# Chunk-selected attention followed by a gated FFN: a hand-merged order against one computed at build time, with VectorE 32x32 transposes in place of TensorE transposes

## The chip, the cores and the metric

The kernel runs on one core of one Trainium2 chip. Times are device microseconds (us) of one execution. "Busy", "waited for" and the chain of waits come from the hardware profile of one execution. Engines in the profile: PE is TensorE's matmuls, PEld its weight loads, DVE is VectorE, ACT is ScalarE, POOL is GpSimd, SP only issues loads and stores. Verdicts come from timed runs taken in turn with the kernel before on the same chip.

## The reference, cut to what matters

Four batches, 8 heads, 768 positions, head size 64. For every query only six of the 24 key chunks (32 keys each) are kept. They are those with the largest upper bound, which is computed from each chunk's minimum and maximum. Attention output goes into a gated FFN.

```python
k_min, k_max = k_chunks.min(3), k_chunks.max(3)          # chunks of 32 keys
ub = sum(max(q * k_min, q * k_max), axis=-1)             # upper bound per query and chunk
ub = where(causal, ub, -1e9);  top = argsort(ub)[..., -6:]
scores = where(selected & (pos_q >= pos_k), q @ k.T / 8, -1e9)
x = softmax(scores) @ v                                   # to (4*768, 512)
out = (sigmoid(x @ w_gate) * (x @ w_val)) @ w_out         # 512 -> 1536 -> 512
```

## The kernel before

The work is cut into eight units: batch 0 to 3, each with a first half "a" and a second half "b" of the queries (384 each). In this text "0b" is the second half of batch 0. Each unit needs preparation (k and q turned so that the head dimension lies on partitions, chunk extremes, bounds, selection), attention, and then the FFN. Preparation of the next unit and the FFN of the previous one are woven into a unit's attention by hand-set fractions; the first unit has a fully hand-written order.

```python
pff = tile_pool(bufs=3, space=PSUM)   # FFN
psc = tile_pool(bufs=3, space=PSUM)   # scores and values
ppr = tile_pool(bufs=2, space=PSUM)   # preparation

def keys_t(u, p, pool, tag="ps"):     # two heads: [positions, 2 x 64] turned by TensorE, fp32
    ps = pool.tile([128, T], F32, ...)
    for x in range(HB):
        nc.tensor.transpose(ps[:, x:T:HB], u.k[:, x, 2*p:2*p+2, :]..., ident32)

def extremes(u, p): ...               # two tensor_reduce per pair, straight from PSUM
def signs(u, p, eng): ...             # max(q,0) and max(-q,0), an own copy for each head
def bounds(u, j):                     # four heads: TensorE into PSUM, ScalarE copies out
def pick(u, j):                       # TensorE turns the bounds (fp32), VectorE: penalty, max8, is_lt
def pick_t(u, j, eng):                # TensorE turns the mask back (fp16), copies into headQ rows 64..95

def score(u, h, x, ...):              # keys carry 32 pattern rows, queries 32 mask rows
    nc.tensor.matmul(ps, headK[...][:, h, ...], headQ[...][:, h, ...])     # 96 rows
    nc.scalar.activation(at, ps, AF.Exp, scale=scale)
    if x == 0: nc.gpsimd.affine_select(...)                                # causal triangle

def merge(a, f):                      # FFN pieces of the previous unit go in by fractions of time
    for c, t in a:
        t(); done_a += c
        while fi < len(f) and done_f + f[fi][0] / 2 <= tf * done_a / ta: ...
# ... cut: opening(), a fixed sequence of about 100 calls for units 0a and 0b
```

The softmax here doesn't subtract the row's maximum and nothing guards it: scores larger than these inputs give would overflow.

Of the kernel before, what the change touches and what calls it, by code (L numbers as in the profile page):

```python
# [14 lines left out]
NEG = -60000.0  # L15


@with_exitstack
def kernel(
# [11 lines left out]
    ctx.enter_context(tc.manual_schedule(engines={nc.gpsimd.engine, nc.sync.engine}))  # L31
# [5 lines left out]
    T = 128 * HB  # L37
    NP = H // 2
# [4 lines left out]
    consts = ctx.enter_context(tc.tile_pool(name="consts", bufs=1))  # L43
    keep = ctx.enter_context(tc.tile_pool(name="keep", bufs=1))
    loads = ctx.enter_context(tc.tile_pool(name="loads", bufs=2))
    nat = ctx.enter_context(tc.tile_pool(name="nat", bufs=1))
    sel = ctx.enter_context(tc.tile_pool(name="sel", bufs=1))
    ubp = ctx.enter_context(tc.tile_pool(name="ubp", bufs=2))
    attp = ctx.enter_context(tc.tile_pool(name="attp", bufs=4))
    small = ctx.enter_context(tc.tile_pool(name="small", bufs=3))  # L50
    xnatp = ctx.enter_context(tc.tile_pool(name="xnatp", bufs=2))
    xtp = ctx.enter_context(tc.tile_pool(name="xtp", bufs=2))
    gatep = ctx.enter_context(tc.tile_pool(name="gatep", bufs=3))
    hglp = ctx.enter_context(tc.tile_pool(name="hglp", bufs=18))
    outp = ctx.enter_context(tc.tile_pool(name="outp", bufs=3))
    PS = bass.MemoryType.PSUM
    pff = ctx.enter_context(tc.tile_pool(name="pff", bufs=3, space=PS))
    psc = ctx.enter_context(tc.tile_pool(name="psc", bufs=3, space=PS))
    ppr = ctx.enter_context(tc.tile_pool(name="ppr", bufs=2, space=PS))

    class Unit:
        def __init__(self, b, half):
            self.b, self.half = b, half
            self.name = f"{b}{'ab'[half]}"
            self.qa, self.qb = HB * half, HB * half + HB
            self.rows = slice(T * half, T * half + T)
            self.sel0 = 1 - half
            self.m = HB - self.sel0
            self.paired = b == 0
            self.cb = T // CH * (half + 1)  # L70
            self.banks = HIGH if half else LOW
            self.where = {}
            base = 0
            for bk in self.banks:
                for (jb, i0, n) in bk:
                    for o in range(0, n, 128):
                        self.where[((i0 + o) // 128, jb)] = base + o
                    base += n
            self.width = base
            self.att, self.pv, self.kps, self.qps, self.ubT = {}, {}, {}, {}, {}  # L80
# [10 lines left out]
    ]  # L91
    units = [Unit(b, half) for b in range(B) for half in range(2)]

    def load(u):
        for n, src in (("k", k), ("q", q)):
            t = loads.tile([128, H, HB, D], F32, tag="raw" + n, name=f"raw{n}_{u.name}")
            for j in range(2):
                nc.sync.dma_start(t[:, 4 * j:4 * j + 4], src[u.b, 4 * j:4 * j + 4, u.rows].rearrange(  # L98
                    "h (p x) d -> p h x d", x=HB))
            setattr(u, "raw" + n, t)  # L100
        u.v = loads.tile([128, HB, H, D], F32, tag="v", name=f"v_{u.name}")
        for i in range(HB):
            r = T * u.half + 128 * i
            nc.sync.dma_start(u.v[:, i], v[u.b, :, r:r + 128].rearrange("h p d -> p h d"))  # L104

    def regroup(u, n, parts):
        raw = getattr(u, "raw" + n)
        if not hasattr(u, n):
            setattr(u, n, nat.tile([128, HB, H, D], F32, tag=n, name=f"{n}_{u.name}"))
        t = getattr(u, n)  # L110
        for f, h0, h1 in parts:
            f(t[:, :, h0:h1, :], raw[:, h0:h1].rearrange("p h x d -> p x h d"))  # L112

    ident32 = consts.tile([128, 128], F32, tag="id32")
    ident16 = consts.tile([128, 128], F16, tag="id16")
    epat = consts.tile([32, NC, CH], F16, tag="epat")
    NQ = 2 * HB - 1
    pen = consts.tile([128, NQ, NC], F32, tag="pen")
    kmx = keep.tile([128, NP, 2, 32], F32, tag="kmx", name="kmx")
    kcat, v16s, apt, headK, headQ = [], [], [], [], []  # L120
    for i in range(2):
        kcat.append(keep.tile([128, H, 32], F32, tag=f"kcat{i}", name=f"kcat{i}"))
        headK.append(keep.tile([96, H, S], F16, tag=f"hk{i}", name=f"hk{i}"))
        headQ.append(keep.tile([96, H, T], F16, tag=f"hq{i}", name=f"hq{i}"))
        apt.append(keep.tile([128, HB, 4, 32], F16, tag=f"ap{i}", name=f"ap{i}"))
        v16s.append(keep.tile([128, 2 * HB, H, D + 1], F16, tag=f"v16{i}", name=f"v16{i}"))

    def fill_pattern(i, eng):
        eng.dma_start(headK[i][64:96],
                      epat.rearrange("p c s -> p (c s)").unsqueeze(1).to_broadcast([32, H, S]))  # L130

    def constants():
        make_identity(nc, ident32)
        nc.vector.memset(epat, 0.0)
        nc.gpsimd.affine_select(
            out=epat, in_=epat, compare_op=ALU.not_equal, fill=NEG,
            base=0, pattern=[[-1, NC], [0, CH]], channel_multiplier=1,
        )
        fill_pattern(0, nc.sync)
        nc.vector.memset(kmx, 0.0)  # L140
        nc.vector.memset(pen, 0.0)
        nc.gpsimd.affine_select(
            out=pen, in_=pen, compare_op=ALU.is_ge, fill=-1e9,
            base=128, pattern=[[128, NQ], [-CH, NC]], channel_multiplier=1,
        )
        for i in range(2):
            nc.vector.memset(kcat[i], 0.0)
            nc.vector.memset(apt[i], 0.0)
            nc.gpsimd.memset(v16s[i][:, :, :, D:D + 1], 1.0)
        nc.vector.memset(headQ[0][64:96, :, 0:128], 0.0)  # L150
        nc.vector.tensor_copy(ident16, ident32)

    wg16 = keep.tile([128, 4, D_FF], F16, tag="wg16")
    wv16 = keep.tile([128, 4, D_FF], F16, tag="wv16")
    wo16 = keep.tile([128, NFB, 512], F16, tag="wo16")
# [4 lines left out]
    def load_w(i):  # L160
        lo, hi = 512 * i, 512 * i + 512
        nc.gpsimd.dma_start(wg16[:, :, lo:hi], wgs[:, :, lo:hi])  # L162
        nc.gpsimd.dma_start(wv16[:, :, lo:hi], wvs[:, :, lo:hi])

    def load_wo(i):
        nc.gpsimd.dma_start(wo16[:, 4 * i:4 * i + 4, :], wos[:, 4 * i:4 * i + 4, :])

    def cast_v(u):
        nc.gpsimd.tensor_copy(v16s[u.b % 2][:, u.qa:u.qb, :, 0:D], u.v)  # L169

    def keys_t(u, p, pool, tag="ps"):
        if p == 0:
            if u.paired:
                u.kmm = kmx[:, :, :, T // CH * u.half:T // CH * (u.half + 1)]
            else:
                u.kmm = sel.tile([128, NP, 2, T // CH], F32, tag="kmm", name=f"kmm_{u.name}")
        ps = pool.tile([128, T], F32, tag=tag, name=f"kT_{u.name}_{p}")
        for x in range(HB):
            nc.tensor.transpose(ps[:, x:T:HB],  # L179
                                u.k[:, x, 2 * p:2 * p + 2, :].rearrange("p h d -> p (h d)"), ident32)  # L180
        u.kps[p] = ps

    def extremes(u, p):
        pv = u.kps[p].rearrange("p (c s) -> p c s", s=CH)
        for e, op in enumerate((ALU.max, ALU.min)):
            nc.vector.tensor_reduce(out=u.kmm[:, p, e, :], in_=pv, op=op, axis=AX.X)  # L186

    def chunks_t(u, j):
        c0 = T // CH * u.half
        for e in range(2):  # L190
            for i, sign in enumerate((1.0, -1.0)):
                nc.vector.tensor_scalar_mul(kcat[u.b % 2][64 * i:64 * i + 64, 4 * j + e:4 * j + 4:2, c0:c0 + T // CH],  # L192
                                            u.kmm[64 * e:64 * e + 64, 2 * j:2 * j + 2, i, :], sign)

    def keys_f(u, p, eng):
        ps = u.kps.pop(p)
        for e in range(2):
            eng(headK[u.b % 2][0:64, 2 * p + e, u.rows], ps[64 * e:64 * e + 64])  # L198

    def queries_t(u, p, pool, tag="ps"):  # L200
        if p == 0:
            u.qs = sel.tile([128, H, T], F32, tag="qs", name=f"qs_{u.name}")
        ps = pool.tile([128, T], F32, tag=tag, name=f"qT_{u.name}_{p}")
        for x in range(HB):
            nc.tensor.transpose(ps[:, x:T:HB],
                                u.q[:, x, 2 * p:2 * p + 2, :].rearrange("p h d -> p (h d)"), ident32)
        u.qps[p] = ps
# [373 lines left out]
```

## Time and profile before

Median of the first three runs: 357.51 us (355.94 to 359.78).

| reading | value |
|---|---|
| profiled span | 353.9 us |
| PE busy | 316.5 us, 89% |
| ACT, DVE, POOL busy | 234.4, 216.4, 74.1 us |
| PE busy in the first 60 us | 41.4 us |

The page's part 1 gives busy time, share and instructions of each engine; part 2 cuts the span in 40 slices and gives the busy share in tenths; part 4 gives the chain that ended last, by engine.

```profile
span 353.9 us, 7200 instructions
PE 316.5 (89%) x2736; PEld 197.0 (56%) x2736; DVE 216.4 (61%) x642; ACT 234.4 (66%) x501; POOL 74.1 (21%) x106
...
PE   4678687999988999999987999999998999999995
...
DVE  6576548985667569864776469883585574322430
...
DMA  8999992057900066001740039001100020001002
...
PE 54%; ACT 16%; issue 10%; DVE 8%; DMA 5%; SPq 4%; POOL 2%; ACTq 0%; POOLq 0%; DVEq 0%
```

The windows view gives busy us in each stretch, with the granted TensorE clock and the DMA engines' share.

```profile
core 0: us, PE busy (x) PEld busy (x) DVE busy (x) ACT busy (x) POOL busy (x), PEclk, DMA share, GB/s
0.00:60.00 60.00, 41.38 (x332) 26.50 (x333) 37.77 (x124) 35.12 (x76) 21.74 (x35) 0.94 1.04 211
60.00:340.00 280.00, 265.11 (x2359) 165.81 (x2358) 177.20 (x516) 196.53 (x420) 52.34 (x72) 1.00 0.23 63
340.00:354.00 14.00, 10.03 (x50) 4.69 (x48) 1.43 (x3) 2.77 (x5) 0.00 (x0) 0.95 0.15 56
```

The timeline of PE, around the first FFN matmul of unit 0a and the first scores of unit 0b (start, duration, engine, line, operation):

```profile
30.40 0.33 PE L330 MATMUL g_0a_512<-xT_0a,wg_120 128*128 128x384 f16 x1
...
55.67 0.39 PE L289 MATMUL sc_0b_0_777<-hq_117,hk_111 96*128 96x128 f16 x4
```

PE is the limit, yet busy PE is not streaming PE. Matmuls overlap and wait while they count as busy: one of 128x384 counts 326 ns, but the next can start 162 ns after it. I therefore count streaming (the time that the matmuls would take one right behind the other) by the medians of start-to-start times (162 ns for a 128x384 matmul, 216 for 128x512, 29 for 128x65, 110 for an fp32 transpose). By that estimate about 286 of the 354 us are streaming. The first 60 us hold 30 us of it.

### The profile page before, as it was taken

The page shows a single profiled execution, that of the slowest core. Times are in us where ns is not written, and L with a number is a line of the kernel's source. Part 1 is how long each engine was busy: PE and PEld are TensorE (multiplying, and loading weights), DVE is VectorE, ACT ScalarE, POOL GpSimd, SP SyncE. Part 2 cuts the span into 40 slices and gives each one's busy share as a digit, 9 for nine tenths or more (in the row PEclk, how much of TensorE's full clock was granted, in tenths as well). Part 3 has the DMA queues.
Part 4 walks back from the last instruction along what each step waited for, and adds up shares of the span by engine and source line. Part 5 has one row for each costly group of instructions (what it writes and reads, how often), then busy time and mean ns, then how long its engine had stood idle before and what let it go on. Part 6 is the DMA issues. An engine that isn't in the chain of part 4 may idle for free.

```text
span 353.9 us, 7200 instructions
## 1 busy us (share of the span) xinstructions
PE 316.5 (89%) x2736; PEld 197.0 (56%) x2736; DVE 216.4 (61%) x642; ACT 234.4 (66%) x501; POOL 74.1 (21%) x106
## 2 busy tenths in 40 slices
PE   4678687999988999999987999999998999999995
PEld 3265345656554566655664466665665456665552
DVE  6576548985667569864776469883585574322430
ACT  4683467787888475876789375884789467665321
POOL 3393204211420040210421032201421011110000
PEclk9979999999999999999999999999999999999999
DMA  8999992057900066001740039001100020001002
GB/s 223 268 207 224 232 226 49 0 163 198 267 3 0 31 199 130 2 0 62 222 77 0 32 113 215 3 0 52 41 0 2 0 87 4 2 3 59 31 0 89
DMA packets 50642, 31.13 MB, mean 88 GB/s; under 512 B 26032, under 2 KB 47536, under 8 KB 50608
## 3 DMA queue, kind: packets, MB, share of 16 engines
q1 hardware_dynamic: 45856, 25.96, 28.2%
q0 software_dynamic: 4752, 4.72, 7.8%
q8 instruction: 21, 0.34, 0.4%
q14 instruction: 13, 0.11, 0.1%
HBM read 28.31 MB, written 6.29 MB: 98 GB/s over the span
## 4 chain that ended last, share of the span: by engine, by line
PE 54%; ACT 16%; issue 10%; DVE 8%; DMA 5%; SPq 4%; POOL 2%; ACTq 0%; POOLq 0%; DVEq 0%
DMA v_0b<-in_v_dram 5%; SPq L104 2%; ACT hq_117 L236 2%; SPq L98 1%; ACT hq_112 L236 1%; ACT qs_2b L227 1%; ACT qs_3b L227 1%; ACT qs_1b L227 1%; ACT hk_116 L198 1%; PE o_2b_4225 L345 1%; PE o_1b_2989 L345 1%; PE o_1a_2399 L345 1%; ACT qs_1a L227 1%; PE o_2a_3645 L345 1%; PE o_0b_1743 L345 1%
## 5 line engine op out<-in xcount | busy, mean ns | idle before, releaser
L336 PEld LDWEIGHTS <-wv_121 128*128 128x128 f16 x384 | 37.0, 97 | 38.4 <-issue 16.6
L330 PEld LDWEIGHTS <-wg_120 128*128 128x128 f16 x384 | 35.2, 98 | 16.1 <-issue 1.9
L289 PEld LDWEIGHTS <-hk_111 96*128 96x128 f16 x240 | 19.7, 101 | 13.0 <-issue 8.2
L289 PEld LDWEIGHTS <-hk_116 96*128 96x128 f16 x240 | 19.2, 97 | 9.4 <-issue 3.1
L179 PE MATMUL kT_0a_172<-ident_105,k_0a 128*128 128x128 f32 x3 | 0.9, 430 | 4.9 <-DVE k_0a L112 4.9
L295 POOL TENSOR_SCALAR_AFFINE_SELECT att_0b_776<-att_0b_776 128x384 f16<-128x384 f16 x1 | 0.5, 515 | 19.7 <-ACT att_0b_776 L292 19.7
L179 PEld LDWEIGHTS kT_0a_172<-ident_105,k_0a 128*128 128x128 f32 x3 | 0.5, 213 | 4.8 <-issue 4.8
L277 ACT COPY hq_117<-apT_0b_735 32x384 f16<-32x384 f16 x4 | 1.9, 469 | 1.8 <-PE apT_0b_735 L273 1.8
L112 ACT COPY k_0a<-rawk_0a 128x384 f32<-128x384 f32 x2 | 1.0, 512 | 2.9 <-DMA rawk_0a<-in_k_dram 2.9
L192 DVE TENSOR_SCALAR kcat_110<-kmm_2b 64x24 f32<-64x24 f32 x8 | 2.8, 350 | 0.1
L192 DVE TENSOR_SCALAR kcat_115<-kmm_3b 64x24 f32<-64x24 f32 x8 | 2.8, 350 | 0.1
L313 DVE RECIPROCAL rz_3b_4888<-pv_3b_4849 128x6 f32<-128x6 f32 x1 | 0.2, 196 | 4.3 <-PE pv_3b_4849 L309 4.3
L277 DVE COPY hq_112<-apT_3a_3801 32x256 f16<-32x256 f16 x4 | 1.2, 288 | 2.7 <-PE apT_3a_3801 L273 2.7
L277 DVE COPY hq_112<-apT_2a_2555 32x256 f16<-32x256 f16 x4 | 1.2, 288 | 2.7 <-PE apT_2a_2555 L273 2.7
L169 POOL CAST v_114<-v_0b 128x1536 f16<-128x1536 f32 x1 | 1.5, 1465 | 6.1 <-DMA v_0b<-in_v_dram 6.1
L313 DVE RECIPROCAL rz_1b_2434<-pv_1b_2339 128x6 f32<-128x6 f32 x1 | 0.2, 196 | 4.0 <-PE pv_1b_2339 L309 4.0
L313 DVE RECIPROCAL rz_2b_3680<-pv_2b_3585 128x6 f32<-128x6 f32 x1 | 0.2, 197 | 4.0 <-PE pv_2b_3585 L309 4.0
L273 PEld LDWEIGHTS <-ap_118 128*128 128x128 f16 x20 | 1.7, 98 | 1.5 <-DVE ap_118 L267 0.2
L162 POOL DMA_DIRECT2D wg_120<-in_moe_w_gate_dram x3 | 2.4, 808 | 0.0
L348 ACT ACTIVATE osb_3b_5093<-o_3b_5080 128x512 f32<-128x512 f32 x1 | 0.6, 597 | 2.8 <-PE o_3b_5080 L345 2.8
L198 ACT CAST hk_111<-kT_0b_494 64x384 f16<-64x384 f32 x2 | 0.9, 474 | 2.2 <-DVE kmx L186 2.2
L169 POOL CAST v_114<-v_0a 128x1536 f16<-128x1536 f32 x1 | 1.5, 1469 | 4.4 <-DMA v_0a<-in_v_dram 4.4
(1976 smaller groups left out, 1085.3 us busy)
## 6 DMA issues: line engine op xcount, KB each, us to landing
wg_120<-in_moe_w_gate_dram POOLq DMA_DIRECT2D x3, 512.0 KB, 8.9
wv_121<-in_moe_w_val_dram POOLq DMA_DIRECT2D x3, 512.0 KB, 12.0
wo_122<-in_moe_w_out_dram POOLq DMA_DIRECT2D x3, 512.0 KB, 13.6
rawk_0a<-in_k_dram SPq DMA_DIRECT2D x2, 384.0 KB, 3.8
rawq_0a<-in_q_dram SPq DMA_DIRECT2D x2, 384.0 KB, 5.2
v_0a<-in_v_dram SPq DMA_DIRECT2D x3, 256.0 KB, 6.3
rawk_0b<-in_k_dram SPq DMA_DIRECT2D x2, 384.0 KB, 6.3
rawq_0b<-in_q_dram SPq DMA_DIRECT2D x2, 384.0 KB, 6.5
```

The costliest lines, as they stand in the source:

```text
L98: nc.sync.dma_start(t[:, 4 * j:4 * j + 4], src[u.b, 4 * j:4 * j + 4, u.rows].rearrange("h (p x) d -> p h x d", x=HB))
L104: nc.sync.dma_start(u.v[:, i], v[u.b, :, r:r + 128].rearrange("h p d -> p h d"))
L169: nc.gpsimd.tensor_copy(v16s[u.b % 2][:, u.qa:u.qb, :, 0:D], u.v)
L192: nc.vector.tensor_scalar_mul(kcat[u.b % 2][64 * i:64 * i + 64, 4 * j + e:4 * j + 4:2, c0:c0 + T // CH], u.kmm[64 * e:64 * e + 64, 2 * j:2 ...
L198: eng(headK[u.b % 2][0:64, 2 * p + e, u.rows], ps[64 * e:64 * e + 64])
L227: nc.scalar.activation(o, src, AF.Relu, scale=sign)
L236: eng(headQ[u.half][0:64, 2 * p + e, :], ps[64 * e:64 * e + 64])
L277: eng(headQ[u.half][64:96, 4 * j + i, s0:T], ps[32 * i:32 * i + 32, s0:T])
L289: nc.tensor.matmul(ps[:, o:o + w], headK[u.b % 2][:, h, 128 * jb:128 * jb + 128], headQ[u.half][:, h, i:i + w], start=True, stop=True)
L330: nc.tensor.matmul(gp, wg16[:, c, 128 * fb:128 * fb + 128], u.xT[:, c, :], start=(c == 0), stop=(c == 3))
L336: nc.tensor.matmul(vp, wv16[:, c, 128 * fb:128 * fb + 128], u.xT[:, c, :], start=(c == 0), stop=(c == 3))
L345: nc.tensor.matmul(op, hgl[(u.name, fc)][:, 128 * tb:128 * tb + 128], wo16[:, fc, :], start=(fc == 0), stop=(fc == NFB - 1))
```

## The change

It keeps the arithmetic and replaces how the work is ordered and turned.

1. Every operation is put into a plan with its reads, writes, buffers, possible engines and a cost for each. At build time a simulation of the engines picks what is issued next, and on which engine. The eight PSUM banks are shared by need.
2. Head p is paired with head p+4. Bounds of eight heads are computed at once into two banks.
3. The selection is turned by VectorE 32x32 block transposes instead of TensorE.
4. In batches 2 and 3 k and q are loaded as 32x32 blocks in 128-byte runs and turned by VectorE. Batches 0 and 1 still use TensorE.

The core of it, cut:

```diff
-    pff = tile_pool(bufs=3)   psc = tile_pool(bufs=3)   ppr = tile_pool(bufs=2)
+    plan = Plan({"ps": 8, "big": 2, "six": 4, ...},
+                {("ps", "ff"): 4, ("ps", "sc"): 3, ("ps", "pv"): 2, ("ps", "pr"): 3})
+def act(n, psum=True, parts=128): took = (170 if psum else 195) + n / 1.2; ...
+def dve(n, rate=1, parts=128):    took = 158 + n / 0.96 / rate; ...
+def pool(n):                      took = 190 + n / 1.2; ...
+  def order(self):     # earliest possible start first, then rank
+      key = (s > free[e], s if s > free[e] else 0.0, op.prio)
+    self.wide = b <= 1                      # batches 2 and 3: blocks
-    nc.tensor.transpose(ps[:, x:T:HB], u.k[...], ident32)
+    nc.vector.transpose(at(u.qf)[:, p], at(raw)[:, p, c0:c0 + NT]...)     # 32x32 blocks
+    nc.vector.tensor_reduce(out, src, op, axis=AX.X, apply_transpose=True)
-    nc.tensor.transpose(ps[...], u.ubT[j][...], ident32)                  # selection
+    nc.vector.transpose(at(ubn)[:, e_]..., at(ub[e_]))
+    hkp{i}{e_}: {DVE: (880, 960)} if i == 0 else {POOL: (2700, 2750)}     # pattern rows into the keys
-    fill_pattern(i): eng.dma_start(headK[i][64:96], epat...)
+    hqm: {POOL: pool(u.n), DVE: dve(u.n, 4, 32), ACT: act(u.n, False, 32)}  # mask rows into the queries
+    for op in plan.order(): op.emit(op.engine)
  # ... cut: the classes, constants, loads, attention and FFN written as plan entries
```

## The prediction

> **What bounds the kernel now.** The tensor engine. The page gives PE 316.5 us busy of a 353.9 us span (89%), against ACT 234.4, DVE 216.4, POOL 74.1; the chain that ended last is 54% PE. From the medians of start-to-start times in the trace (gate and value matmuls 128x384: 162 ns; output 128x512: 216; values 128x65: 29; fp32 transposes 110; fp16 transposes 55) I count about 286 us of pure streaming for all 2736 matmuls (an estimate; FFN alone 186). So about 68 us are lost: some 29 us in the first 60 us (windows view: PE 41.4 busy, granted clock 0.94, DMA engines saturated; POOL waits 19.7 us for the first 0b scores, which start only at 55.7 us, long after 0a's FFN began), some 36 us over 60-340 us (PE 265 busy of 280, about 244 streaming), 4 us in the tail.
>
> **What leaves PE** (estimates from those pitches): k and q transposes of batches 2 and 3, 96 x 109 ns = 10.5 us; selection's transposes, 40 x 110 + 40 x 55 ns = 6.6 us; the bounds stay near 10 us. Streaming falls to about 268 us. FFN, scores and values stay.
>
> **Other engines.** DVE loses sign splits, chunk sign copies and key casts, and gets 32x32 transposes, which I cost like its other ops of one element per cycle (549 ns at 384). It ends near 170 us fixed work plus a share of copies. The Trainium skill ("VectorE: DVE Perf Modes", The three transpose paths) says that this transpose turns 32x32 blocks only and goes to SBUF; no run shows its time yet. ACT keeps about 166 us that cannot move (exp 105, tanh 47, output 14). POOL roughly doubles, to 130-170 us. None becomes the bound. A risk: "GPSIMD Engine Reference" (Key points) says that POOL shares its SBUF interfaces with VectorE in two-port modes, so POOL copies might stretch (now 1.46 us for 1536).
> DMA: batch 2-3 k and q come in 128-byte runs, 49,152 packets; from 22 ns at 256 B and 36 ns at 768 B I estimate 18 ns each, 55 us of all 16 engines, at 100-250 us where they are mostly idle.
>
> **Order.** Half or more of the gain should come from order: PSUM banks shared as needed, copies on whichever engine is free, 0b's attention beginning when its data is there. I expect the first 60 us to lose 22 instead of 29, and the steady part 22 instead of 36, since real waits differ from the model's fixed costs; tail 4. Sum: 268 + 22 + 22 + 4 = 316; 2 more for POOL and DVE collisions.
>
> **Prediction: 318 us, 302 to 338 with 8 chances in 10.** Faster by over 2%: 0.94; within 2%: 0.03; slower: 0.03.
>
> **What would show the steps.** Matmuls drop from 2736 to about 2650, fp32 transposes from 232 to 96. From 60 us on PE is busy over 95%. 0b's first scores start before 45 us. POOL over 120 us. DVE transposes near 0.5 us per 384 columns. 128-byte packets near 18 ns.
>
> **What would make it wrong.** In-order queues obey an order computed from fixed costs: where a POOL copy or a DMA is late, PE stalls behind it and the gains of order vanish (335-345). DVE could bind if transposes are slower than one element per cycle. If the order nearly fills PE from 25 us on, 300 is possible. The start could be worse, since the first selection now needs eight heads' keys and queries.

## The result, and the profile after

The changed kernel took 319.65 us (median of four; 319.46 to 320.87). The kernel before took 356.73 us beside it. The ratio is 0.8961, with a 95% interval of 0.8917 to 0.9004. A ratio here is the mean time of one kernel's fast runs over that of the other's of the same rounds, so not quite the ratio of the medians quoted.

The same lines of the page:

```profile
span 317.8 us, 7014 instructions
PE 289.7 (91%) x2656; PEld 181.5 (57%) x2656; DVE 198.9 (63%) x568; ACT 206.4 (65%) x440; POOL 104.1 (33%) x171
...
PE   3577789989999949999998999999999999999995
...
DVE  8988694498868999678999617432675213321420
...
DMA  7999999704999357998410010000200010002002
...
PE 63%; DVE 19%; ACT 11%; issue 3%; DMA 2%; POOL 1%; SPq 0%; ACTq 0%; DVEq 0%; POOLq 0%
```

The windows view, and the timeline of PE around the same two matmuls:

```profile
0.00:60.00 60.00, 44.78 (x360) 28.04 (x361) 45.47 (x137) 44.07 (x97) 32.31 (x51) 0.94 1.11 232
60.00:304.00 244.00, 234.75 (x2251) 148.73 (x2249) 151.86 (x429) 159.59 (x339) 71.81 (x120) 0.99 0.36 64
304.00:318.00 14.00, 10.18 (x51) 4.76 (x49) 1.58 (x3) 2.77 (x5) 0.00 (x0) 0.98 0.16 57
```

```profile
40.90 0.65 PE L679 MATMUL g_0a<-xT_0a,wg 128*128 128x384 f16 x3
...
47.04 0.55 PE L593 MATMUL sc_0b<-hqe,hke 96*128 96x128 f16 x5
```

Three things are to be seen. From 60 us to the tail PE is busy 234.75 of 244 us (96%, before 95%). More of it is streaming: by the same count 275 us in all, of which 33 lie in the first 60 us and 228 in the 240 us from 60 to 300. In the last ten slices but the very last PE is simply full, while VectorE is down to 0 to 5 tenths. But the start has hardly gained: 33 us of streaming in 60 us against 30. Unit 0b's scores begin 9 us earlier, and 0a's FFN begins 10 us later. VectorE now stands in the chain of waits with 19% instead of 8%.

The VectorE transposes cost what other fp32 work of that size costs on VectorE: in the same trace its reductions of 384 columns from PSUM take 547 ns in the mean (groups by form; after the first bar stand the busy us of the group and the mean ns of one):

```profile
L489 DVE STREAM_TRANSPOSE kt<-k 128x768 f16<-128x768 f16 x8 | 7.6, 944 | 0.0
...
L503 DVE STREAM_TRANSPOSE qf_2a<-q 128x384 f32<-128x384 f32 x4 | 2.1, 552 | 0.0
```

### The profile page after: what moved, and what is told of

Its sections match the earlier page's. It is cut to its first block, busy times and chain, and to the rows that moved or that the text cites. A ratio compares the mean times of both kernels' runs of the same rounds, so it can differ in the third digit from the quotient of the medians.

```text
span 317.8 us, 7014 instructions
## 1 busy us (share of the span) xinstructions
PE 289.7 (91%) x2656; PEld 181.5 (57%) x2656; DVE 198.9 (63%) x568; ACT 206.4 (65%) x440; POOL 104.1 (33%) x171
## 4 chain that ended last, share of the span: by engine, by line
PE 63%; DVE 19%; ACT 11%; issue 3%; DMA 2%; POOL 1%; SPq 0%; ACTq 0%; DVEq 0%; POOLq 0%
PE o_2a L700 2%; PE o_1b L700 2%; PE v_3a L679 2%; PE g_3a L679 2%; PE g_2a L679 2%; PE v_2a L679 2%; PE v_3b L679 2%; PE g_3b L679 2%; PE o_3b L700 2%; PE o_2b L700 2%; PE o_3a L700 2%; PE g_0a L679 2%; PE v_0a L679 2%; PE v_2b L679 2%; PE g_2b L679 2%
## 5 line engine op out<-in xcount | busy, mean ns | idle before, releaser
L679 PEld LDWEIGHTS <-wv 128*128 128x128 f16 x384 | 36.4, 98 | 21.7 <-issue 1.8
L679 PEld LDWEIGHTS <-wg 128*128 128x128 f16 x384 | 35.1, 97 | 17.9
L593 PEld LDWEIGHTS <-hke 96*128 96x128 f16 x240 | 19.3, 101 | 13.5 <-issue 7.5
L593 PEld LDWEIGHTS <-hko 128*128 128x128 f16 x240 | 18.6, 99 | 7.5 <-DVE x_0a L648 0.8
L607 ACT ACTIVATE att_1b<-sc_1b 128x512 f16<-128x512 f32 (+1 forms) x32 | 16.7, 578 | 1.7 <-PE sc_1b L593 1.6
L607 ACT ACTIVATE att_3b<-sc_3b 128x512 f16<-128x512 f32 (+1 forms) x32 | 17.0, 580 | 1.2 <-PE sc_3b L593 1.2
L607 ACT ACTIVATE att_2b<-sc_2b 128x512 f16<-128x512 f32 (+1 forms) x32 | 17.0, 580 | 0.9 <-PE sc_2b L593 0.8
L607 ACT ACTIVATE att_0b<-sc_0b 128x512 f16<-128x512 f32 (+1 forms) x32 | 16.5, 625 | 0.9 <-PE sc_0b L593 0.7
L679 PE MATMUL g_0a<-xT_0a,wg 128*128 128x384 f16 x48 | 9.9, 326 | 0.1
L700 PE MATMUL o_0b<-wo,hg_0b 128*128 128x512 f16 x36 | 9.9, 435 | 0.0
L613 POOL TENSOR_SCALAR_AFFINE_SELECT att_3a<-att_3a 128x384 f16<-128x384 f16 x8 | 4.2, 521 | 17.6 <-ACT att_3a L607 17.5
```

Source lines behind the costliest of these rows:

```text
L593: nc.tensor.matmul(at(t)[:, o:o + w], hk[u.par][e_][USED[e_], p, 128 * jb:128 * jb + 128], hq[u.half][e_][USED[e_], p, i:i + w], start=Tru ...
L607: plan.add(f"exp_{u.name}_{h}_{x}", {ACT: act(n)}, lambda e, t=t, att=att, b0=b0, n=n: nc.scalar.activation(at(att)[:, b0:b0 + n], at(t), ...
L613: nc.gpsimd.affine_select(out=dv, in_=dv, compare_op=ALU.is_ge, fill=0.0, base=0, pattern=[[0, HB], [1, 128]], channel_multiplier=-1)
L679: nc.tensor.matmul(at(t), w16[:, c, 128 * fb:128 * fb + 128], at(u.xt)[:, c, :], start=(c == 0), stop=(c == 3))
L700: nc.tensor.matmul(at(o), at(hgs[fc])[:, 128 * tb:128 * tb + 128], wo16[:, fc, :], start=(fc == 0), stop=(fc == NFB - 1))
```

## The experiments

Twelve kernels ran, all correct. They answer three questions: how the gain divides between less TensorE work and order, which part of the ordering carries it, and why the start did not gain.

### 1. Less work or better order: undo the work alone

The three edits keep the simulated order. The first puts batches 2 and 3 back on TensorE (with the four large buffers under names of their own, since sharing them left the plan no way on). The second writes the selection with TensorE transposes again. The third does both.

```diff
# x1_pe_layout
-            self.wide = b <= 1
+            self.wide = b <= 3
-  "six": 4                      + "kn": 1, "qn": 1, "qf": 1, "qm": 1
# x2_pe_select (cut; per bank of four heads, as in the kernel before)
-  nc.vector.transpose(ubn, ub)                 # from PSUM, 32x32 blocks
+  copy(ubt, ub);  for x in range(m): nc.tensor.transpose(ubp[...], ubt[...], ident32)
-  nc.vector.transpose(apt, ap)
+  for x in range(m): nc.tensor.transpose(apt[...], apq[...][:, x], ident16)
# x3_pe_both: both edits
```

> The changed kernel with one part undone: batches 2 and 3 get their k and q layout by TensorE transposes again, like batches 0 and 1; order still from the build-time simulation. Theory of the prediction (work on the tensor engine is worth its streaming time): 96 fp32 transposes x 109 ns = 10.5 us more, so about 330 us. Rival 'worth more' (the block layout mostly relieves the other engines and PSUM): 336 us or more. Rival 'order is all' (the tensor engine has slack to take it): 322 us or less.

> The changed kernel with the selection turned by TensorE again: bounds copied out of PSUM, 40 fp32 transposes, bounds and maxima as before, 40 fp16 transposes, mask rows from PSUM; order still from the simulation. Theory of the prediction: 6.6 us of streaming, so about 326 us. Rival 'worth more': 330 us or more. Rival 'order is all': 321 us or less.

> Both parts undone at once: all of the tensor engine's removed transposes are back, only the simulated order, the shared PSUM banks, the free choice of engine and the pairing of heads remain of the change. Theory of the prediction (work worth 17 us, order worth 20): about 337 us. Rival 'worth more': over 345 us, order alone brings little. Rival 'order is all': under 326 us.

| run | median us | ratio to before (95%) | what it undoes |
|---|---|---|---|
| the change | 319.65 | 0.8961 (0.8917 to 0.9004) | |
| x1_pe_layout | 325.38 | 0.9099 (0.9034 to 0.9164) | layout: 5.7 us |
| x2_pe_select | 325.56 | 0.9104 (0.9044 to 0.9165) | selection: 5.9 us |
| x3_pe_both | 335.38 | 0.9377 (0.9322 to 0.9433) | both: 15.7 us |

With all removed TensorE transposes back, 21.6 of the gain remain (356.97 less 335.38). So order and what comes with it (shared banks, free engines, pairing, finer copies) is worth about 22 us, and the removed transposes about 16. Both rivals fall: order is not all, and work is not worth far more than its streaming. The layout alone, though, cost only 5.7 us to undo where 10.5 us of streaming came back. The windows of the two traces show where the rest was; each first number is PE busy, the third DVE busy, in the same 20 us. First the change, then x1_pe_layout:

```profile
100.00:120.00 20.00, 15.82 (x138) 8.67 (x136) 19.86 (x60) 11.69 (x27) 8.59 (x14) 0.98 0.54 121
```

```profile
100.00:120.00 20.00, 19.77 (x176) 11.98 (x173) 17.95 (x62) 12.32 (x30) 8.27 (x17) 1.00 0.69 181
```

In the change VectorE is full there (19.86 of 20 us), about half of it with batch 2's keys and queries, and PE stands idle for 4 us; with TensorE doing that layout PE is full. That is a reading of two traces; experiment 4 tests it.

### 2. Which part of the ordering carries the gain

```diff
# x4_by_rank: same operations, next one by fixed rank alone; engine that would end it first
-  best = earliest possible start over all engines, then rank
+  best = lowest rank of all operations whose buffers are free
# x5_static_psum
-  {"ps": 8, ...}, caps ff 4, sc 3, pv 2, pr 3
+  {"ff": 3, "sc": 3, "pr": 2, ...}             # scores and values share the middle three
# x6_flat
+  engines = {e: (400, 500) for e in engines}    # one cost for everything but loads
# x7_fixed_engine
+  if len(engines) > 1: engines = {ACT or DVE in turn: its cost}
```

> The changed kernel, same operations, but emitted by fixed rank alone (the interleaving by fractions that feeds the simulation), without regard to simulated readiness; each operation still goes to the engine that would end it first. If the simulated readiness is what fills the tensor engine: clearly slower than the change, 345 us or more. If finer pieces, shared banks and fewer transposes suffice: about 325 us.

> The changed kernel with the eight PSUM banks split fixedly as before (3 for the FFN, 3 for scores and values, 2 for preparation), order re-simulated under that limit. If sharing banks is a large part of what order brings: 328 us or more. If the order itself carries the gain: within 3 us of the change, 319 to 323 us.

> The changed kernel ordered by the same simulation, but with every operation given the same cost (400 ns busy, 500 ns to its end) on every engine; loads keep their modelled times. If the measured costs in the model matter: 330 us or more. If knowing only what waits for what, with ranks and free engines, suffices: within 5 us of the change.

> The changed kernel with each movable copy put to a fixed engine, ScalarE and VectorE in turn (VectorE or ScalarE alone where it can't be the other), none on GpSimd where ScalarE or VectorE can do it; order simulated with that. If the free choice of engine is a large part: 330 us or more. If not: 320 to 325 us; it could even gain, since GpSimd then collides less with VectorE.

| run | median us | ratio to before (95%) |
|---|---|---|
| x4_by_rank | 363.79 | 1.0169 (1.0101 to 1.0238) |
| x5_static_psum | 326.58 | 0.9130 (0.9067 to 0.9193) |
| x6_flat | 345.09 | 0.9622 (0.9553 to 0.9691) |
| x7_fixed_engine | 321.99 | 0.8986 (0.8928 to 0.9044) |

The same operations by fixed rank are 44 us slower than the change, and 1.7% slower than the kernel before with all its extra work (interval 1.0 to 2.4%). In that trace PE waits for single late copies, up to 8.4 us for one, and what was emitted behind it waits too; in the change its longest single wait is 4.2 us (who waited for whom, total us, times, longest):

```profile
PE xps_2a L641 <- DVE x_2a L633: 10.1, 4, 8.4
PE sc_0b L578 <- DVE hqe L237: 5.5, 1, 5.5
```

So fewer transposes and finer pieces brought nothing under this order; an order that knows when inputs are ready is needed to collect them. (The rank order is not the hand-made order of before, which was tuned; the run doesn't say what that order lacked.) Knowing only what waits for what is not enough either: flat costs lose 25 us. Part of both losses may lie in the clock. Its mean in the profiled executions is 0.939 with the rank order and 0.949 with flat costs, against 0.983 in the change. The shortfall from full clock, times the span, is 22, 18 and 5 us, so by an estimate at most 17 of the 44 us and 12 of the 25 us lie there; whether the order brought the lower clock about was not tested. Sharing the banks is worth some 7 us; this lies between the two figures expected, so it is a real but not a large part. Free choice of engine is worth little: 2.3 us in the medians, and the intervals of the ratios overlap.

### 3. Why the start did not gain

In the change two long GpSimd copies run at the start. They write the chunk pattern into the keys of the odd batches, which are needed only at 80 us. VectorE's timeline of the change beside GpSimd's; the second column is the duration:

```profile
8.66 0.97 DVE L453 TENSOR_TENSOR kcr<-kx_0a,kcr 128x12 f32<-128x12 f32 x1
...
10.49 1.94 DVE L453 TENSOR_TENSOR kcr<-kx_0a,kcr 128x12 f32<-128x12 f32 x1
```

```profile
6.87 2.74 POOL L254 COPY hke<-epat 32x3072 f16<-32x3072 f16 x1
9.67 2.74 POOL L254 COPY hko<-epat 64x3072 f16<-64x3072 f16 x1
```

A subtraction of 12 elements takes 0.15 to 0.16 us with no GpSimd work beside it (x8_late_fill below, at 8.54 and 9.60). During the copies it took 0.97 and 1.94 us, and it ended at 9.63 and 12.43 us, within 0.03 us of the copies' ends (9.61 and 12.41). The Trainium skill ("SBUF — State Buffer", SBUF: two separate sides) describes this: VectorE and GpSimd share one pair of ports under an exclusive lock, held for a whole instruction, against VectorE ops with two SBUF inputs or in a two-port mode. This trace agrees. The other side can wait too: in x8_late_fill a GpSimd copy of 384 elements that began during a VectorE copy of the pattern (5.18 to 6.56 us) took 1.32 us, where others of its kind take 0.51. In the change both subtractions stand in the chain that ended last, with 2.75 us together (start, us, what):

```profile
8.75 0.89 DVE kcr L453
...
10.57 1.86 DVE kcr L453
```

```diff
# x8_late_fill
-  hkp1: two GpSimd copies of 3072 elements, as soon as GpSimd is free
+  hkp1: eight copies of 768 elements, after unit 0b's values are cast
# x10_late_noqm: x8, and
-  qm of batches 2 and 3: {DVE, ACT, POOL: pool(2 * u.n)}
+  qm of batches 2 and 3: {DVE, ACT}
# x11_recal: x10, and four VectorE costs from the trace of the change
-  hqm: dve(u.n, 4, 32)    kcr: dve(n)        hk: dve(S, 4, 64)      qm: dve(2 * u.n, 2)
+  hqm: dve(u.n, 1.55, 32) kcr: (257, 337)    hk: dve(S, 2.37, 64)   qm: dve(2 * u.n)
# x0_control: the change, unedited
```

> The changed kernel once more, unedited, as the yardstick on this chip for the three runs beside it: 319.7 us as before, within 1 us.

> The changed kernel, but the two long GpSimd copies of the chunk pattern into the keys of odd batches (2.7 us each, at 6.9 and 9.7 us) are cut in eight and wait until the values of unit 0b are cast, some 20 to 40 us later; the model's order of all else stays the same. Theory (two VectorE subtractions of 12 elements took 0.97 and 1.94 us because they waited for those copies): each ends near 0.15 us, the first selection comes 2 to 3 us earlier, and the whole is 2 to 3 us faster. Rival (the start hangs on loads or on the selection's length): no change beyond 1 us.

> As the run before, and GpSimd may not take the maxima with zero of the queries of batches 2 and 3, which took it 1.5 and 2.1 us where the model says 0.6 and 0.8. One of these stood in the chain of waits at 126.8 us. Theory: 1 to 2 us faster than the run before. Rival (slack takes it up): no change.

> As the run before, and four VectorE costs of the model set to the means measured in the trace of the change (mask rows 417 ns for 384 columns instead of 268, the 12-element subtraction 337 instead of 170, half-partition fp16 key copies 495 instead of 368, maxima of queries at one element per cycle). Theory (the model's optimism about VectorE makes it overload VectorE between 60 and 160 us): 2 to 4 us faster than the run before. Rival (the shape of the order matters, not its numbers): within 1 us.

| run | median us | ratio to before (95%) |
|---|---|---|
| x0_control | 320.99 | 0.8985 (0.8958 to 0.9012) |
| x8_late_fill | 313.22 | 0.8767 (0.8733 to 0.8801) |
| x10_late_noqm | 312.74 | 0.8767 (0.8740 to 0.8794) |
| x11_recal | 309.34 | 0.8670 (0.8645 to 0.8696) |

Moving two copies brought 7.8 us in the medians, more than the 2 to 3 us expected. The profiled spans, 317.8 and 312.7, differ by only 5.1 us, but they pair an execution of the change at a clock of 0.983 with the slowest one of x8_late_fill, at 0.978. At like clocks, 0.987 to 0.988, the control took 319.52 us and x8_late_fill 311.36 and 310.78. The control came out 1.3 us above its earlier median, a little outside what was expected of it. The four subtractions of unit 0a all took 0.15 to 0.16 us, three of them here:

```profile
8.54 0.15 DVE L454 TENSOR_TENSOR kcr<-kx_0a,kcr 128x12 f32<-128x12 f32 x1
...
9.60 0.16 DVE L454 TENSOR_TENSOR kcr<-kx_0a,kcr 128x12 f32<-128x12 f32 x1
...
11.12 0.16 DVE L454 TENSOR_TENSOR kcr<-kx_0a,kcr 128x12 f32<-128x12 f32 x1
```

The mask of unit 0a is turned at 19.0 us instead of 23.2, 0a's FFN starts at 36.3 instead of 40.9, and 0b's scores at 43.0 instead of 47.0. PE's timeline of x8_late_fill shows the last two:

```profile
36.34 0.50 PE L680 MATMUL g_0a<-xT_0a,wg 128*128 128x384 f16 x2
...
43.00 0.38 PE L594 MATMUL sc_0b<-hqe,hke 96*128 96x128 f16 x4
```

In the profiled executions that gain of 4 to 5 us is kept to the end. By the chain above about 2.4 us of it is the wait of the two subtractions (2.75 less two of 0.16; an estimate). Part of the rest is that GpSimd, now free, took five of the eight early copies of 0a's k and q, where it had taken one and ScalarE seven. So the run shows what the two copies cost, but does not split their lock from GpSimd's time.

One thing more differs at the start, and no run isolates it. The first fp32 transposes on PE start 213 ns apart, later ones 109. The slow rate ends at 7.8 us in the kernel before and near 12 us in x8_late_fill, but only at about 20 us in the change, where the bounds of 0a ran at it too (0.63 us each, against 0.38 to 0.40). The clock column does not show this. It may be a part of the start's loss, and of x8_late_fill's gain.

Keeping GpSimd from the query maxima gave nothing, so that the chain passed through one of them was not a cost. They are slow on GpSimd all the same (instructions of that source line in the change; duration in ns, min, median, max):

```profile
L477 POOL TENSOR_SCALAR qm_2a<-qf_2a x1: 1496/1496/1496, 120.0 to 120.0; 128x512 f32<-128x512 f32 x1
L477 POOL TENSOR_SCALAR qm_2b<-qf_2b x1: 2126/2126/2126, 126.8 to 126.8; 128x768 f32<-128x768 f32 x1
```

Correcting four costs in the model to what the trace of its own kernel shows brought another 3.4 us in the medians. About 1 us of that may be clock: x10_late_noqm had 0.973 to 0.978 in five of its six executions, x11_recal 0.987 to 0.994 in all, and at 0.987 they took 311.85 and 309.33 us. In the profiled executions of x8_late_fill and x10_late_noqm the clock is at half for 6.8 us from 111 us on, in x11_recal it is not; whether the better costs avoid that was not tested. The four costs were changed together; which of them counts is not known.

### 4. Was the VectorE layout held back by the order?

```diff
# x12_recal_pe_layout: x11_recal with
-            self.wide = b <= 1
+            self.wide = b <= 3
```

> The recalibrated run (309.3 us) with the layout of batches 2 and 3 back on TensorE. Undoing that part cost the unedited change only 5.7 us for 10.5 us of streaming. Theory: the VectorE layout paid for itself only in part there, because VectorE was the bound around 100 to 120 us under the optimistic order; with the recalibrated order nothing is given back, and undoing it costs the full streaming, 319 to 321 us. Rival (the VectorE work of that layout costs its 4 to 5 us under any order): 314 to 316 us.

It took 320.20 us, a ratio of 0.8957 (0.8931 to 0.8983): 10.9 us above x11_recal, where the same edit had cost 5.7 us in the unedited change. So the VectorE layout is worth the whole streaming that it takes from TensorE, once the order gives it room; about half of that was being given back (up to 1.7 us of it by the clock, which in both traces of the change is at half for 3.4 us from 119 us on, and not there in the three others of this comparison). The windows from 60 to 120 us agree. PE busy (first number) is 52.71 us in the change and 56.26 in x11_recal, with the same VectorE load. First the change, then x11_recal:

```profile
60.00:120.00 60.00, 52.71 (x543) 34.01 (x541) 50.88 (x149) 41.53 (x95) 23.25 (x42) 0.99 0.69 110
```

```profile
60.00:120.00 60.00, 56.26 (x509) 34.76 (x509) 50.96 (x145) 43.96 (x98) 25.88 (x46) 1.00 0.89 146
```

Since x11_recal holds three edits, the run says that they freed the layout's worth together, not which did.

## Why the prediction was right or wrong

**The time and its two halves: right.** 318 us were predicted and 319.65 measured. That the total came out within 2 us is in part luck, as the terms below show. Of the predicted gain 17 us were put down to removed TensorE work and 20 to order. Undoing the work cost 15.7 us, and 21.6 us remained with it undone. What bounds the kernel was read correctly: where PE is full, streaming is paid one for one (selection: 6.6 us estimated, 5.9 measured; layout: 10.5 estimated, 10.9 measured in the recalibrated order).

**What was counted: right.** 2656 matmuls (about 2650 predicted), 96 fp32 transposes, a 384-column fp32 transpose on VectorE at 0.55 us, 128-byte packets at 17.5 ns in the mean (18 predicted, though from medians, and their median is 13), and none of these loads in the chain that ended last. Over the stretch from 60 us to the end PE is busy 95.0% (244.9 of 257.8 us, from the windows), just at the line drawn.

**"Streaming falls to about 268 us": mis-sized.** The same count gives 275 for the change. All but the bounds fell from 276 to 259 us, the 17 us that were predicted. The bounds, which were to stay near 10 us, grew in this count to about 16, since 160 fp32 matmul instructions became 256. PE time that only they cover fell from 16.2 to 14.8 us, so the count is a poor measure of these small overlapping matmuls, and they did not get dearer.

**"I expect the first 60 us to lose 22 instead of 29": wrong.** They lose 27 (60 less 33). The first scores of 0b, expected before 45 us, start at 47.0. The failing step was to take the start's loss for a matter of order, where the prediction only named the eight-head selection as a risk. The runs show two long GpSimd copies in the way: without them the first 60 us stream 36 us, and 0b's scores start at 43.0. That 0a's FFN still starts later than before (36.3 against 30.4 us) fits the named risk that a first selection now needs all eight heads. That rest was not tested, nor was the slow rate of PE in the first 20 us (experiment 3).

**"The steady part 22 instead of 36": mis-sized the other way.** From 60 to 300 us PE streams 228 of 240 us, so 12 us are lost. The errors of start, streaming and steady part cancelled in the sum, which is luck.

**"2 more for POOL and DVE collisions": too small.** Moving two copies alone brought 8 us in the medians, of which about 2.4 are the collision itself (estimate in experiment 3). The direction named was only half of it: POOL copies were expected to stretch. In the change they hardly do (a copy of 768 elements in 64 partitions took 0.82 to 0.83 us, once 0.90), and VectorE is the one that waits; in x8_late_fill one POOL copy did stretch, from 0.51 to 1.32 us.

**"POOL over 120 us": wrong, 104.1.** I had put more of the free copies there than the simulation chose. Nothing hung on it: with none of the movable copies on GpSimd (x7_fixed_engine) the time is almost the same.

## What to carry to other kernels

An order computed at build time is only as good as its costs: with one cost for all it lost 25 us, and feeding four measured durations back into it together gained 3.4 us (2.5 at like clocks), so profile the scheduled kernel and correct the model. Taking work off the full engine pays its streaming time only if the engine that takes the work over is not full just then; look at both engines in the stretch where the work lands. Keep long GpSimd instructions away from a chain of short VectorE ops that others wait for, as at the start here; a constant that is needed late should not be written as soon as an engine is free.

## What the Trainium skill lacked or had wrong

- "GPSIMD Engine Reference" (Engine selection) calls one-input elementwise work on GpSimd roughly line-rate. Here a GpSimd maximum with a constant, fp32, took 1.50 us for 512 (1.47 to 1.50 in other runs' traces, once 1.87) and 2.13 us for 768 elements per partition, about 2.5 ns for each further element ((2126 - 1496) / 256), while an fp32-to-fp16 GpSimd cast of 512 took 0.61 us in the median.
- "VectorE: DVE Perf Modes" (The perf-mode tier table) has no row for the 32x32 transpose; the skill gives its rate and one 16-bit time elsewhere, but no times by type and size. In the change fp16 ran no faster than fp32: 709 and 954 ns in the mean for 512 and 768 fp16 elements of the mask (0.96 ns for each further element), 429 and 544 ns for 256 and 384 fp32 elements of the bounds (0.90 ns). A reduction with a built-in transpose took 951 ns for 768 fp32 elements.
- "SBUF — State Buffer" has the port lock right, as the traces show (VectorE's held subtractions end within 0.03 us of the GpSimd copies). "GPSIMD Engine Reference" (Key points), read alone, speaks of contention only and leaves open that a 0.15 us VectorE op can be held for 1.94 us.
